# Half of a causal mask moved from VectorE to ScalarE and GpSimd, and a split pair of the last layer put in one buffer

## The chip, the cores and the metric

The kernel runs on one core of one Trainium2 chip. The metric is the device time of one launch in microseconds (us); lower is better. The engines are TensorE (PE, with its weight loads as PEld), VectorE (DVE), ScalarE (ACT), GpSimd (POOL) and SyncE (SP), which issues most DMAs. SBUF is the memory that the engines work in, PSUM the one that TensorE writes.

## The reference, cut to what matters

```python
# 1. linear attention with a decaying state: B, H, S, D = 4, 8, 768, 48
for t in range(S):
    state = alpha[:, :, t, :, None] * state + einsum('bhd,bhe->bhde', k[:, :, t], v[:, :, t])
    y[:, :, t] = einsum('bhd,bhde->bhe', q[:, :, t], state)
# 2. mixture of experts, top 1 of 8: D = 384, F = 1024, N = B*S = 3072 tokens
out[mask] = gate_w[mask, None] * (maximum(x[mask] @ w1[e], 0.0) @ w2[e])
# 3. maxout layer, width 768
return maximum(maximum(x @ w1, x @ w2), x @ w3) @ w_out
```

## The kernel before, in words

Everything runs in one launch, in three stages. In each, the order of the instructions on every engine is the order in which the program text issues them (a manual schedule); what crosses from one engine to another waits on semaphores.

**Attention.** The 3072 tokens are cut into 24 groups `g` of 128 tokens; six groups make one batch, and the state `sbar` is carried from group to group within a batch. The decay is handled by two running products per group, computed on VectorE by scans: `undo` (L290) for the keys and `decay` (L303) for the queries. `decay` then has GpSimd multiply the queries by the product (L305, 112x512, written back to `qt`), and `keys` has VectorE multiply the keys (L316). `spread` (ACT, L311) copies the scaled queries into a block-diagonal tile. `scores(g, hf)` multiplies keys and queries on TensorE for half of the head pairs (`hf` 0 and 1, one PSUM bank `sc` each, 128 keys by 4 heads by 128 queries); `causal(g, hf)` copies this to SBUF as `ss` and sets it to zero where the key comes after the query: one VectorE multiplication by `mask` of 128x512 per half (L345). `sv(g, hf)` multiplies `ss` by the values (L366); `qs(g)` adds what the state gives (L375); `kback` and `update` form the next state, of which VectorE does an addition (L410) and a multiplication (L413), two instructions each. `xev` reads the result (L387 on DVE, L388 and L390 on ACT); `ranges` (ACT, L320) is a check of the products' size.

The loop body of iteration `g` issues, for a later group each: `sv(g, 0)`, `undo(g+3)`, scatters, `sv(g, 1)`, `values(g+2)`, `kback(g+1)`, `spread(g+2)`, `decay(g+3)`, then for both halves `scores(g+1, hf)` and `causal(g+1, hf)`, then `ranges(g+1)`, `keys(g+2)`, `qs(g)`, `xev(g)`, `update(g)`, scatters. So VectorE's order is: scan L290, reciprocal L297, scan L303, both L345, L316, L387, L410, L413. GpSimd's order is: `tokens` (L381, a small copy), a scatter, the query product L305, a scatter. From group 8 on the scatters (L498, indirect DMAs that GpSimd writes) send finished token rows to memory, sorted by expert.

Every second to fourth group a routing chain `route` picks the experts of finished tokens in small VectorE steps spread over an iteration; its one-hot comparison (`oh`, L433) comes right behind `causal`, and TensorE's ranking matmuls (L438) wait for it. In groups 12 to 20 every second iteration also splits expert weights into a rounded part and a rest (`split_w`: ACT L231, L232, POOL L234, DVE L235).

**Experts** (from about 171 us): TensorE multiplies the sorted tokens by each expert's weights, with each operand as a sum of two parts.

**Last layer** (from about 404 us). `x2T` is cut into `BLOCKS` of 256, five times 512, and 256 tokens. `up2(i, f)` computes one of six slices of the hidden layer of block `i`: three groups of nine matmuls (L937 to L939), a copy on ACT (L941), two maxima on DVE (L943), a rounded part `fh` on ACT (L945) and the rest `fl` on GpSimd (L946). `down2(i, q)` multiplies 128 tokens of block `i` by the output weights `wo` (L954 to L956) and scatters the rows (L960). The down part of block `i` runs between the up parts of block `i+1`. The output weights come as 64-bit numbers and are converted by `convert`, a chain of 18 steps (6 weights of 3 steps, L820 to L836 on DVE, ACT and POOL) which are taken two at each `f` of block 0 and three at each `f` of block 1; `down2(0, q)` follows `up2(1, 2)`.

Of the kernel before, what the change touches and what calls it, by code (L numbers as in the profile page):

```python
# [10 lines left out]
F32R = mybir.dt.float32r  # L11
# [4 lines left out]
ALU = mybir.AluOpType  # L16
# [6 lines left out]
C = 128  # L23
# [8 lines left out]
NF2 = F2 // 128  # L32
# [10 lines left out]
TB = 512  # L43
# [16 lines left out]
def fused_kernel(ctx, tc, qT, kT, aT, vn, vf, emb, tau, w1, w2, m1, m2, m3, mo,  # L60
                 gq, gk, ga, gv, out):
    nc = tc.nc
# [75 lines left out]
    for i in range(2):  # L138
        t = wk.tile([HR, WE], F32, tag=f"first{i}", name=f"first{i}", bufs=1)
# [3 lines left out]
    for i in range(3):  # L143
        t = wk.tile([HR, NP, 2, C], F32, tag=f"bdq{i}", name=f"bdq{i}", bufs=1)
# [4 lines left out]
    mask = cst.tile([128, 128], F32, name="mask")  # L149
    nc.gpsimd.memset(mask, 1.0)  # L150
    nc.gpsimd.affine_select(mask, mask, pattern=[[1, 128]], compare_op=ALU.is_ge, fill=0.0,
                            base=0, channel_multiplier=-1)
    sbars = []
    for i in range(2):
        t = wk.tile([HR, H * DE], F32, tag=f"sbar{i}", name=f"sbar{i}", bufs=1)
# [185 lines left out]
    def causal(g, hf):  # L341
        t = cur[g]
        sc = t["sc", hf]
        ss = wk.tile([128, 4, C], F32, tag="ss", name=f"ss_{g}_{hf}", bufs=4)
        nc.vector.tensor_mul(ss, sc.rearrange("p i j t -> p (i j) t"), mask.unsqueeze(1).broadcast_to([128, 4, C]))  # L345
        t["ss", hf] = ss

    def kback(g):
# [145 lines left out]
    def step(it):  # L494
        return next(it, None)
# [131 lines left out]
    with tc.manual_schedule():  # L627
# [18 lines left out]
        embedding_turn(esq)  # L646
        spread(1)
        causal(0, 0)
        causal(0, 1)
        wx = ps_x.tile([128, 512], F32, tag="xp", name="wx")  # L650
        warm(wx, NWARMX)
# [13 lines left out]
        for g in range(NT):  # L665
# [34 lines left out]
            if g + 1 < NT:  # L700
                for hf in range(2):
                    scores(g + 1, hf)
                    causal(g + 1, hf)
                ranges(g + 1)
# [104 lines left out]
    def read_m(src, f):  # L809
        n = f"{src.tensor.name}_{f}"  # L810
        rawm[n] = cvs[-1].tile([128, DM, 2], I32, tag="cr", name=f"cr_{n}", bufs=2)
        nc.sync.dma_start(rawm[n], src[:, f])
# [25 lines left out]
    def convert(ws):  # L838

        for n, w in enumerate(ws):  # L840
            if n + 1 < len(ws):
                read_m(*ws[n + 1][:2])
            for _ in load_m(*w):
                yield
            yield
# [8 lines left out]
    def block(i, pool):  # L854

        w, o = BLOCKS[i], sum(BLOCKS[:i])
        shape = [128, KD, w if i == 0 else TB]
        xh = pool.tile(shape, F32R, tag="bxh", name=f"bxh_{i}")[:, :, 0:w]
        xl = pool.tile(shape, F32R, tag="bxl", name=f"bxl_{i}")[:, :, 0:w]
        for k in range(KD):  # L860
            src = x2T[:, k, o:o + w]
            nc.scalar.copy(xh[:, k], src)
            nc.vector.tensor_sub(xl[:, k], src, xh[:, k].bitcast(F32))
        xsp[i] = (xh, xl)

    with tc.manual_schedule():
        gate_steps = gates()
        conv = convert(todo)
        for s, (u, c) in enumerate(order + [(NU, None)]):
            if s < NA:  # L870
                continue
            e, f = divmod(u, NF1)
# [31 lines left out]
            if e + 1 < E:  # L904
                if u == 1:
                    fetch(1)
                f0 = 5 if e == 0 else 4
# [13 lines left out]
    f2 = fctx.enter_context(tc.tile_pool(name="f2", bufs=2))  # L921
# [7 lines left out]
    def up2(i, f):  # L929
        xh, xl = xsp[i]  # L930
        w = BLOCKS[i]
        t0 = f2.tile([128, TB], F32, tag="t0", name=f"t0_{i}_{f}")[:, 0:w]
        for n in range(3):
            pt = ps_p[n].tile([128, TB], F32, tag="p", name=f"p_{i}_{f}_{n}")[:, 0:w]
            m = mws[n][f]
            for k in range(KD):
                nc.tensor.matmul(pt, m[:, 0, k], xh[:, k], start=(k == 0), stop=False)  # L937
                nc.tensor.matmul(pt, m[:, 1, k], xh[:, k], start=False, stop=False)  # L938
                nc.tensor.matmul(pt, m[:, 0, k], xl[:, k], start=False, stop=(k == KD - 1))  # L939
            if n == 0:  # L940
                nc.scalar.copy(t0, pt)  # L941
            else:
                nc.vector.tensor_tensor(t0, pt, t0, op=ALU.max)  # L943
        hh, hl = (f2.tile([128, TB], F32R, tag=n, name=f"{n}_{i}_{f}", bufs=NF2 + 3)[:, 0:w] for n in ("fh", "fl"))
        nc.scalar.copy(hh, t0)  # L945
        nc.gpsimd.tensor_sub(hl, t0, hh.bitcast(F32))  # L946
        hsp[i, f] = (hh, hl)

    def down2(i, q):
        sl = slice(q * 128, (q + 1) * 128)  # L950
        op = ps_o.tile([128, DM], F32, tag="o", name=f"o_{i}_{q}")
        for f in range(NF2):
            hh, hl = hsp[i, f]
            nc.tensor.matmul(op, hh[:, sl], wo[f][:, 0], start=(f == 0), stop=False)  # L954
            nc.tensor.matmul(op, hh[:, sl], wo[f][:, 1], start=False, stop=False)  # L955
            nc.tensor.matmul(op, hl[:, sl], wo[f][:, 0], start=False, stop=(f == NF2 - 1))  # L956
        t = sum(BLOCKS[:i]) // 128 + q
        ot = f2.tile([128, DM], F32, tag="ot", name=f"ot_{t}", bufs=3)
        nc.scalar.activation(ot, op, AF.Copy, scale=gts[:, t:t + 1])
        nc.gpsimd.indirect_dma_start(out=out, out_offset=bass.IndirectOffsetOnAxis(ap=idx[:, t, 0:1], axis=0),  # L960
                                     in_=ot, in_offset=None, bounds_check=N - 1, oob_is_err=False)

    with tc.manual_schedule():
        nc.sync.dma_start(idx.bitcast(I32), meta[0:N].rearrange("(t p) o -> p t o", p=128))
        nc.vector.memset(gts, 0.0)
        read_m(*todo_o[0][:2])
        block(1, f2)
        conv = convert(todo_o)
        for i in range(NB + 1):
            for f in range(NF2):  # L970
                if i < NB:
                    up2(i, f)
                if i < NB and f < BLOCKS[i] // 128:
                    for t in (sum(BLOCKS[:i]) // 128 + f,):
                        nc.gpsimd.indirect_dma_start(
                            out=gts[:, t:t + 1], out_offset=None, in_=gtok,
                            in_offset=bass.IndirectOffsetOnAxis(ap=idx[:, t, 1:2], axis=0),
                            bounds_check=N - 1, oob_is_err=False)
                for _ in range(2 if i == 0 else 3 if i == 1 else 0):
                    step(conv)  # L980
                if i > 0:
                    f0 = f - 2 if i == 1 else f
                    for q in range(max(0, 2 * f0), min(2 * f0 + 2, BLOCKS[i - 1] // 128)):
                        down2(i - 1, q)
                if f == 3 and 1 < i + 1 < NB:
                    block(i + 1, f2)
        okr = nc.values_load(okv[0:1, 0:1], min_val=0, max_val=128,  # L987
                             skip_runtime_bounds_check_because="a count of 128 flags")
# [159 lines left out]
```

## Time and profile before

| | |
|---|---|
| median of 3 runs (lowest to highest) | 718.27 us (718.24 to 719.01) |
| the profiled execution: its time, its span | 718.81 us, 717.1 us |
| PE, PEld busy | 694.2 us (97%), 634.3 us (88%) |
| DVE, ACT, POOL busy | 433.3 us (60%), 281.8 us (39%), 297.6 us (41%) |

The page cuts the span into 40 slices of 17.9 us; each digit is the busy share in tenths, and PEclk is the granted clock of TensorE in tenths of full speed:

```profile
PE   8999999999999999999999999999999999999994
DVE  8899999897378788888998697211311311303110
ACT  3656566464345444544455323211211212212221
POOL 5312655543124454554555267332333233243331
PEclk9999999899999999999999999999999999999998
```

Slices 0 to 8 are the attention, 9 to 21 the experts, the rest the last layer. A row of a timeline gives start and length in us, engine, line and operation, the tile written and the tiles read, and in brackets how long the engine sat idle before it and what ended that. Consecutive equal instructions are merged (x2), and their lengths overlap a little, since an engine starts the next one before the last has written all. An instruction that is held up after its start shows a greater length, not an idle time.

### The profile page before, as it was taken

The numbers are of one execution on the slowest core, as the hardware profiler recorded it, in microseconds if no ns is written. First come the engines' busy times: TensorE is split into PE (matmuls) and PEld (weight loads), VectorE is DVE, ScalarE is ACT, GpSimd is POOL, SyncE is SP. The second block draws the span as 40 slices with busy tenths as digits, with TensorE's granted clock in tenths as the row PEclk, the third lists the DMA queues.
The fourth block names the chain that finished last, engine by engine and source line by source line (L and its number), as shares of the span: only waits on it lengthen the run. The fifth ranks groups of instructions, "written<-read, shape, count | busy, mean of one in ns | idle before, by whom it ended". The sixth has DMA issues, their size and how long they took to land. (4 is left out here: it accounts for less than half of the span.)

```text
span 717.1 us, 11261 instructions
## 1 busy us (share of the span) xinstructions
PE 694.2 (97%) x4098; PEld 634.3 (88%) x4098; DVE 433.3 (60%) x811; ACT 281.8 (39%) x613; POOL 297.6 (41%) x314
## 2 busy tenths in 40 slices
PE   8999999999999999999999999999999999999994
PEld 4899898899988999999999997888888898898994
DVE  8899999897378788888998697211311311303110
ACT  3656566464345444544455323211211212212221
POOL 5312655543124454554555267332333233243331
PEclk9999999899999999999999999999999999999998
DMA  9999978121355547547454220000000000000000
GB/s 241 287 266 297 321 212 271 53 87 67 108 159 169 146 135 216 173 153 213 148 178 131 46 68 23 23 11 34 1 22 23 1 22 23 1 33 12 12 34 25
DMA packets 32687, 79.69 MB, mean 111 GB/s; under 512 B 8808, under 2 KB 10864, under 8 KB 32624
## 3 DMA queue, kind: packets, MB, share of 16 engines
q1 hardware_dynamic: 28752, 69.40, 33.0%
q0 software_dynamic: 3840, 9.48, 3.5%
q8 instruction: 34, 0.56, 0.3%
q14 instruction: 29, 0.24, 0.1%
q10 hardware_dynamic: 32, 0.01, 0.0%
HBM read 66.97 MB, written 11.90 MB: 110 GB/s over the span
## 5 line engine op out<-in xcount | busy, mean ns | idle before, releaser
L943 DVE TENSOR_TENSOR t<-p,t 128x512 f32<-128x512 f32 (+1 forms) x84 | 51.6, 614 | 198.5 <-PE p L939 195.4
L939 PE MATMUL p<-bxl,m 128*128 128x512 f32 (+1 forms) x378 | 137.0, 362 | 0.0
L937 PE MATMUL p<-bxh,m 128*128 128x512 f32 (+1 forms) x378 | 137.0, 362 | 0.0
L938 PE MATMUL p<-bxh,m 128*128 128x512 f32 (+1 forms) x378 | 137.0, 362 | 0.0
L946 POOL TENSOR_TENSOR fl<-t,fh 128x512 fp32r<-128x512 f32 (+1 forms) x42 | 49.1, 1168 | 153.1 <-ACT fh L945 153.1
L234 POOL TENSOR_TENSOR w<-r,w 128x384 fp32r<-128x384 f32 x64 | 72.3, 1132 | 85.2 <-ACT w L231 85.2
L939 PEld LDWEIGHTS p<-bxl,m 128*128 128x128 f32 x378 | 71.1, 188 | 12.3
L938 PEld LDWEIGHTS p<-bxh,m 128*128 128x128 f32 x378 | 71.1, 188 | 12.0
L937 PEld LDWEIGHTS p<-bxh,m 128*128 128x128 f32 x378 | 71.1, 188 | 11.9
L945 ACT CAST fh<-t 128x512 fp32r<-128x512 f32 (+1 forms) x42 | 23.5, 559 | 146.8 <-DVE t L943 146.8
L590 PE MATMUL h<-xh,w 128*128 128x224 f32 (+8 forms) x207 | 72.1, 348 | 0.0
L591 PE MATMUL h<-xh,w 128*128 128x224 f32 (+8 forms) x207 | 70.4, 340 | 0.3 <-POOL w L234 0.3
L592 PE MATMUL h<-xl,w 128*128 128x224 f32 (+8 forms) x207 | 70.1, 339 | 0.0
L235 DVE TENSOR_TENSOR w<-r,w 128x384 fp32r<-128x384 f32 x64 | 60.3, 942 | 13.4 <-ACT w L232 13.3
L620 PE MATMUL y<-hl,w 128*128 128x464 f32 (+8 forms) x192 | 66.4, 346 | 0.0
L618 PE MATMUL y<-hh,w 128*128 128x464 f32 (+8 forms) x192 | 65.9, 343 | 0.0
L619 PE MATMUL y<-hh,w 128*128 128x464 f32 (+8 forms) x192 | 65.9, 343 | 0.0
L305 POOL TENSOR_TENSOR qt<-qt,PR 112x512 f32<-112x512 f32 x24 | 30.3, 1261 | 67.6 <-DVE PR L303 24.8
L600 ACT ACTIVATE hh<-h 128x464 fp32r<-128x464 f32 (+8 forms) x64 | 32.0, 501 | 61.5 <-PE h L592 61.5
L337 PE MATMUL sc<-bdq,kt 112*128 112x256 f32 x192 | 50.8, 412 | 1.1 <-POOL hm L184 1.1
L366 PE MATMUL xp<-vt,ss 128*128 128x56 f32 x384 | 47.1, 276 | 3.8 <-ACT jk L320 2.4
L955 PE MATMUL o<-wo,fh 128*128 128x384 f32 x144 | 48.5, 337 | 1.5 <-POOL wo L836 1.5
(205 smaller groups left out, 1445.9 us busy)
## 6 DMA issues: line engine op xcount, KB each, us to landing
r<-in_w SPq DMA_DIRECT2D x64, 384.0 KB, 3.7
cr_in_m<-in_m SPq DMA_DIRECT2D x18, 384.0 KB, 4.8
at<-in_aT SPq DMA_DIRECT2D x11, 451.9 KB, 10.7
kt<-in_kT SPq DMA_DIRECT2D x11, 448.0 KB, 10.6
qt<-in_qT SPq DMA_DIRECT2D x11, 448.0 KB, 9.1
vt<-in_vn SPq DMA_DIRECT2D x11, 448.0 KB, 7.9
ft<-in_vf SPq DMA_DIRECT2D x11, 384.0 KB, 6.9
exr<-xs_scratch SPq DMA_DIRECT2D x5, 675.5 KB, 7.8
```

The lines of the kernel that those rows point to most:

```text
L234: nc.gpsimd.tensor_sub(a[:, 1], r1[:, k], a[:, 0].bitcast(F32))
L235: nc.vector.tensor_sub(b[:, 1], r2[:, k], b[:, 0].bitcast(F32))
L590: nc.tensor.matmul(hp, a[:, 0, k], t["xh"][:, k, c], start=(k == 0), stop=False)
L591: nc.tensor.matmul(hp, a[:, 1, k], t["xh"][:, k, c], start=False, stop=False)
L592: nc.tensor.matmul(hp, a[:, 0, k], t["xl"][:, k, c], start=False, stop=(k == KD - 1))
L618: nc.tensor.matmul(y, w[:, 0, sl], hh, start=(f == 0 and c.start == 0), stop=False, skip_group_check=True)
L619: nc.tensor.matmul(y, w[:, 1, sl], hh, start=False, stop=False, skip_group_check=True)
L620: nc.tensor.matmul(y, w[:, 0, sl], hl, start=False, stop=(f == NF1 - 1), skip_group_check=True)
L937: nc.tensor.matmul(pt, m[:, 0, k], xh[:, k], start=(k == 0), stop=False)
L938: nc.tensor.matmul(pt, m[:, 1, k], xh[:, k], start=False, stop=False)
L939: nc.tensor.matmul(pt, m[:, 0, k], xl[:, k], start=False, stop=(k == KD - 1))
L943: nc.vector.tensor_tensor(t0, pt, t0, op=ALU.max)
```

## The change: what it does

Two things are changed. First, from group 1 on, the second half of a group's scores (`hf` 1) is no longer multiplied by the mask on VectorE: ScalarE copies the PSUM bank to `ss`, and GpSimd then sets the upper triangle to zero in place by `affine_select`, an operation that keeps an element where an expression of partition and position is not negative. The first half, and both halves of group 0, stay on VectorE. In program order the copy stands on ScalarE between `spread(g+2)` and `ranges(g+1)`, and the selection on GpSimd between the query product of `decay(g+3)` and the next scatter.

Second, in the last layer both parts of the hidden tiles of block 0 (256 columns each) lie in one `fh` tile of 512 columns. `fh` gets 10 buffers where it had 9, `fl` 7 where it had 9. The conversion of the output weights takes two steps at each `f` of block 1 where it took three, and `down2(0, q)` comes behind `up2(1, 3)` where it came behind `up2(1, 2)`.

```diff
--- before.py
+++ after.py
@@ -342,7 +342,13 @@
         t = cur[g]
         sc = t["sc", hf]
         ss = wk.tile([128, 4, C], F32, tag="ss", name=f"ss_{g}_{hf}", bufs=4)
-        nc.vector.tensor_mul(ss, sc.rearrange("p i j t -> p (i j) t"), mask.unsqueeze(1).broadcast_to([128, 4, C]))
+        sc = sc.rearrange("p i j t -> p (i j) t")
+        if hf == 0 or g == 0:
+            nc.vector.tensor_mul(ss, sc, mask.unsqueeze(1).broadcast_to([128, 4, C]))
+        else:
+            nc.scalar.copy(ss, sc)
+            nc.gpsimd.affine_select(ss, ss, pattern=[[0, 4], [1, C]], compare_op=ALU.is_ge, fill=0.0, base=0,
+                                    channel_multiplier=-1)
         t["ss", hf] = ss
 
     def kback(g):
@@ -941,7 +947,11 @@
                 nc.scalar.copy(t0, pt)
             else:
                 nc.vector.tensor_tensor(t0, pt, t0, op=ALU.max)
-        hh, hl = (f2.tile([128, TB], F32R, tag=n, name=f"{n}_{i}_{f}", bufs=NF2 + 3)[:, 0:w] for n in ("fh", "fl"))
+        fh = f2.tile([128, TB], F32R, tag="fh", name=f"fh_{i}_{f}", bufs=NF2 + 4)
+        if 2 * w <= TB and i == 0:
+            hh, hl = fh[:, 0:w], fh[:, w:2 * w]
+        else:
+            hh, hl = fh[:, 0:w], f2.tile([128, TB], F32R, tag="fl", name=f"fl_{i}_{f}", bufs=NF2 + 1)[:, 0:w]
         nc.scalar.copy(hh, t0)
         nc.gpsimd.tensor_sub(hl, t0, hh.bitcast(F32))
         hsp[i, f] = (hh, hl)
@@ -976,10 +986,10 @@
                             out=gts[:, t:t + 1], out_offset=None, in_=gtok,
                             in_offset=bass.IndirectOffsetOnAxis(ap=idx[:, t, 1:2], axis=0),
                             bounds_check=N - 1, oob_is_err=False)
-                for _ in range(2 if i == 0 else 3 if i == 1 else 0):
+                for _ in range(2 if i < 2 else 0):
                     step(conv)
                 if i > 0:
-                    f0 = f - 2 if i == 1 else f
+                    f0 = f - 3 if i == 1 else f
                     for q in range(max(0, 2 * f0), min(2 * f0 + 2, BLOCKS[i - 1] // 128)):
                         down2(i - 1, q)
                 if f == 3 and 1 < i + 1 < NB:
```

## Rows read from the trace of the kernel before

**Rows 1.** Busy us by window: PE, PEld, DVE, ACT, POOL; PEclk, DMA, GB/s
```profile
24.00:160.00 136.00, 129.50 (x1001) 123.20 (x1001) 128.13 (x265) 83.51 (x192) 59.17 (x63) 0.96 0.75 224
122.00:126.00 4.00, 4.00 (x16) 3.41 (x15) 3.84 (x10) 2.58 (x6) 0.25 (x1) 0.57 0.96 357
135.00:143.00 8.00, 8.00 (x38) 7.25 (x38) 5.03 (x13) 3.99 (x9) 6.28 (x7) 0.57 0.28 101
600.00:660.00 60.00, 60.00 (x277) 50.72 (x276) 13.55 (x19) 13.82 (x26) 19.39 (x17) 1.00 0.04 14
```

**Rows 2.** Timeline of VectorE through one group without routing
```profile
34.85 1.29 DVE L345 TENSOR_TENSOR ss<-sc,mask 128x512 f32<-128x512 f32 x2
36.05 0.70 DVE L316 TENSOR_TENSOR kt<-kt,PR 112x512 f32<-112x512 f32 x1
...
38.65 1.23 DVE L290 TENSOR_TENSOR_SCAN PR<-at,last 112x516 f32<-112x516 f32 x1 [0.20 <-DVE sbar L413]
...
40.13 1.23 DVE L303 TENSOR_TENSOR_SCAN PR<-at,first 112x516 f32<-112x516 f32 x1
41.39 1.29 DVE L345 TENSOR_TENSOR ss<-sc,mask 128x512 f32<-128x512 f32 x2
```

**Rows 3.** Timeline of TensorE, the two value products of the same stretch
```profile
36.34 1.90 PE L366 MATMUL xp<-vt,ss 128*128 128x56 f32 x16
...
42.55 1.90 PE L366 MATMUL xp<-vt,ss 128*128 128x56 f32 x16
```

**Rows 4.** Timeline of GpSimd, the query product of the same stretch
```profile
41.44 1.19 POOL L305 TENSOR_TENSOR qt<-qt,PR 112x512 f32<-112x512 f32 x1 [5.23 <-DVE PR L303]
```

**Rows 5.** Timelines of VectorE and GpSimd where a query product came late
```profile
73.67 0.95 DVE L433 TENSOR_TENSOR oh<-fi,sm 128x32 bf16<-128x32 f32 x1
...
80.43 1.18 POOL L305 TENSOR_TENSOR qt<-qt,PR 112x512 f32<-112x512 f32 x1 [2.64 <-PE xp L375]
...
81.33 0.82 DVE L316 TENSOR_TENSOR kt<-kt,PR 112x512 f32<-112x512 f32 x1
```

**Rows 6.** Instructions of line 345: shortest, median, longest ns, first and last start
```profile
L345 DVE TENSOR_TENSOR ss<-sc,mask x48: 675/684/693, 13.4 to 166.7; 128x512 f32<-128x512 f32 x48
```

**Rows 7.** Timelines of GpSimd and VectorE, two GpSimd instructions in a row (experts)
```profile
307.44 1.01 POOL L836 TENSOR_TENSOR m<-v_in_m,v_in_m 128x384 fp32r<-128x384 f32 x1
...
307.56 1.31 DVE L235 TENSOR_TENSOR w<-r,w 128x384 fp32r<-128x384 f32 x1 [0.23 <-ACT w L232]
...
308.41 1.33 POOL L234 TENSOR_TENSOR w<-r,w 128x384 fp32r<-128x384 f32 x1
```

**Rows 8.** Timelines of VectorE and GpSimd, the second of two selections (start)
```profile
3.79 1.71 DVE L290 TENSOR_TENSOR_SCAN PR<-at,last 112x516 f32<-112x516 f32 x1 [0.88 <-DMA at<-in_aT]
...
4.13 0.28 POOL L151 TENSOR_SCALAR_AFFINE_SELECT mask<-mask 128x128 f32<-128x128 f32 x1
```

**Rows 9.** GpSimd by line and form: busy us, mean ns, idle before
```profile
L305 POOL TENSOR_TENSOR qt<-qt,PR 112x512 f32<-112x512 f32 x24 | 30.3, 1261 | 67.6 <-DVE PR L303 24.8 <-DVE sm L431 13.6 <-PE sc L337 8.7
...
L151 POOL TENSOR_SCALAR_AFFINE_SELECT mask<-mask 128x128 f32<-128x128 f32 x1 | 0.3, 283 | 0.0
...
L186 POOL TENSOR_SCALAR_AFFINE_SELECT hm<-hm 128x24 f32<-128x24 f32 x1 | 0.2, 213 | 0.1
```

**Rows 10.** ScalarE by line and form, from 410 to 700 us
```profile
L941 ACT COPY t<-p 128x512 f32<-128x512 f32 x30 | 17.5, 585 | 24.4 <-PE p L939 24.4
```

**Rows 11.** Timeline of TensorE, three of its gaps in the attention
```profile
74.67 0.22 PE L438 MATMUL rk<-oh,ones_b 128*128 128x24 bf16 x3 [0.86 <-DVE oh L433]
...
119.86 1.96 PE L366 MATMUL xp<-vt,ss 128*128 128x56 f32 x16 [0.94 <-issue]
...
134.36 2.39 PE L366 MATMUL xp<-vt,ss 128*128 128x56 f32 x16 [1.09 <-ACT jk L320]
```

**Rows 12.** Timelines of VectorE and TensorE, the last conversion and the first down2
```profile
441.19 1.53 DVE L825 SCALAR_TENSOR_TENSOR ex_in_mo<-ex_in_mo,sg_in_mo 128x384 int32<-128x384 int32 x1
...
446.54 0.44 PE L955 MATMUL o<-wo,fh 128*128 128x384 f32 x1 [1.45 <-POOL wo L836]
```

## The prediction

> **What bounds the kernel now.** I read the slices of the page first: TensorE is busy in nine tenths or more of nearly every slice, VectorE only in the first nine. Then busy time by window, for the attention alone: in 136 us TensorE sits idle for 6.5 (129.50 busy) and VectorE for 7.9 (128.13 busy) [rows 1]. Both are nearly full, so I laid their timelines side by side. With all inputs there, TensorE needs 42.55 - 36.34 = 6.21 us for a group [rows 3], VectorE 41.39 - 34.85 = 6.54 us [rows 2]. VectorE is the slower by 0.33 us, but it starts ahead and skips the state work at the end of each batch; so TensorE runs without a gap for some groups, then meets a VectorE that is late, and waits: 0.86, 0.94 and 1.09 us are three of these waits [rows 11]. After two of them TensorE's granted clock was 0.57 on average, over 4 and over 8 us [rows 1], a mix of 2.4 GHz and a stretch at 1.2; that cost 4 x 0.43 + 8 x 0.43 = 5.1 us of TensorE's work. Behind the attention TensorE sets the time, with one hole in the last layer of 1.45 us, where the first down2 waits for the last converted weights [rows 12].
>
> **The change, VectorE's side.** Call T the end of the L303 scan (41.36) [rows 2]. Before, the two masks run from T+0.03, 0.645 us each (half of 1.29), the keys L316 from T+1.23 to T+1.93 (34.82 to 36.05 and 36.75) [rows 2]. 23 masks of 0.645 us leave VectorE, 14.8 us in all. If that came free, VectorE's group would take 5.9 us and TensorE's 6.21 would rule.
>
> It does not come free. GpSimd's query product starts at T+0.08 and lasts 1.19 [rows 4]: it lies exactly beside the two masks. The masks never felt it, 675 to 693 ns in all 48 [rows 6]; their scores come from PSUM. The keys, whose operands are both in SBUF, do feel it: where the product came late (80.43 to 81.61), they took 0.82 us instead of 0.70 and ended 0.54 us after the product's end; the one-hot comparison, also with two SBUF operands, once took 0.95 [rows 5]. So with one mask gone the keys are issued at T+0.65, stand until the product (T+0.08 to T+1.27) is nearly through and end at 1.27 + 0.54 = T+1.81. VectorE wins 0.12 us a group, not 0.645. 21 of the 23 selections have a query product ahead of them; of these one iteration waits for TensorE anyway and in two the product came late; 18 x 0.12 = 2.2 us.
>
> The Trainium skill, page "SBUF — State Buffer", section "Who interferes with whom", has this as a rule against the change: a VectorE instruction with two SBUF inputs and a GpSimd instruction that reads SBUF share one read interface, and whichever comes second waits for the whole of the first. The trace agrees, by the 0.82 us above. By the rule the gain is the 2.2 us; without it TensorE's limit would rule and the 6.5 us of idle time could go.
>
> **The other engines.** ScalarE gets 23 copies of 128x512 from PSUM; the same form costs 0.585 us [rows 10], 13.5 us in all. The scores' second half is complete before T in a group that VectorE limits, so the copy is done before GpSimd has finished the query product. Behind it on ScalarE wait L320, which nobody on the path needs, and L388, which waits for VectorE anyway; ScalarE is busy 83.5 of 136 us [rows 1]. I cost it at nothing; if L388 came late, the 0.6 us would go to a scatter.
>
> GpSimd gets 23 selections of 128x512. The trace has none of that size: 0.213 us for 24 columns and 0.283 for 128 [rows 9], 0.67 ns a column, so 0.283 + 384 x 0.67 ns = 0.54; four times the 128 columns gives 1.13, the two-operand product of nearly this size 1.19 [rows 4]. I take 0.6, nearest to the same operation's own slope, and keep 0.54 to 1.19. The selection reads SBUF too. In the one clean case of VectorE waiting while GpSimd had a second instruction right behind the first, VectorE went between: L235 waited for L836 and ended at 308.87, and L234, issued at 308.41, took 1.33 instead of about 1.0 [rows 7]. So the selection comes after the keys' reads, from T+1.67 to T+2.27, beside L387 and L410, which read PSUM. GpSimd's queue behind it (scatter, `tokens`, the weight rest of split groups, scatter) moves back 1.0 us at most; it is busy 59 of 136 us [rows 1], and 14 us more leave it room before the next query product.
>
> **TensorE's side.** In a group that VectorE limits, the first half of `sv` starts at about T+0.85 and the second at T+1.8; now the second waits for the selection, T+2.3. So such a gap moves by VectorE's accumulated gain less 0.5 us. Group by group: the gap before group 6 gives +0.1 (VectorE ahead by 0.4 to 0.5 after routing in group 4). In group 8, where a late product held the one-hot comparison (the 0.95 us of rows 5), that hold goes and I put VectorE 1.1 us earlier; the gap before group 11 then gives -0.6, before 16 -0.9, before 18 -1.1, the last one-hot wait -0.4 more. Sum: about -1.5 us of the 2.2. The clock's two low stretches I leave as they are.
>
> **Last layer.** Six conversion steps now spread over three `f` of block 1 instead of two, and their user comes one up2 later. The last two steps took 441.19 to 446.54, 5.35 us [rows 12]; the last pair now starts when `up2(1, 2)` is through, and TensorE has `up2(1, 3)` (27 matmuls) and 15 of down2 to do first, 42 x 60/277 = 9.1 us [rows 1]. The 1.45 us go, and nothing on TensorE's path behind gives them back: -1.45. The bounds are 0 (another wait takes its place) and -1.45. The new buffers: `fh` holds six of block 0 and four of block 1, so `up2(1, 4)` finds one free as down2 of block 0 is done by then. With 7 `fl` GpSimd has to wait at `up2(i, 1)` until `down2(i-1, 3)` has begun; behind it are gathers and scatters with a whole block to spare. Nothing.
>
> **Sum.** On the profiled execution: 718.81 (span 717.1 and 1.7 around it) - 1.5 - 1.45 = 715.9. The median shown is 0.54 lower: 715.3 us. Its own range is 713.5 to 717.2: attention -0.3 to -3.3.
>
> **Rivals.**
> *GpSimd keeps the read port (slower).* If the selection follows the product at once, the keys stand until T+1.27+0.54+0.6 = T+2.35, 0.42 later than before; 18 groups give +7.6, with -1.45 that is 724.4 us. For it: the first scan of the kernel took 1.71 us instead of 1.23, ending at 5.50, so it started 0.14 before the end of the second of two selections in a row [rows 8]; it had let both pass. Against it: rows 7, and that this scan's start may not be the time at which it asked. Each group that goes this way costs 0.54 against the forecast; from the sixth of 18 the kernel is no faster than before.
>
> *TensorE runs through (faster).* If shorter waits keep the clock up, the 5.1 us come back: 710.2. For it: the low stretches follow the longest waits of all, and the one of 0.86 was followed by none (slice 4 of the page). Against: the waits only shrink by half a microsecond or move between the two halves of `sv`. If VectorE also got its 0.645 us, the 6.5 us of idle time would go and 705 is the floor.
>
> *The selection is long (no change).* With 1.19 us it ends at T+2.86. From a group's first `sv` to the second half two groups on, TensorE needs 6.21 + 0.87 = 7.1 us; VectorE takes 41.36 - 36.75 = 4.6 us from its keys to T [rows 2], so the selection would end 4.6 + 2.9 = 7.5 us after the state product: some 0.4 us per two groups in the stretches without gaps, some 2 us, and 0.6 at each gap. Attention +1.5, in all 718.3 us.
>
> **Chances.** Forecast 0.46, GpSimd keeps the port 0.22, TensorE runs through 0.19, long selection 0.13. About 0.2% (1.44 us) is what a measurement can tell from no change, so "faster" is below 716.83: nearly all of the forecast (0.41), the fast rival (0.19) and 0.02 of the long selection, 0.62; within 0.2% the rest of the forecast and most of the long selection, 0.15; slower 0.23. The range 709 to 722 takes in the fast rival's 710.2 and two thirds of the way to the slow one's 724.4.
>
> **What would show it.** L316 longer than 0.9 us from its issue, ending 0.5 us after L305: the port. L345 at 25 instead of 48, 0.68 each. The selection starting as L316 ends: right; L316 ending 0.5 us after the selection: the slow rival. Idle time of TensorE inside `sv`, ahead of its second eight matmuls. Windows from 120 to 143 us at clock 1.0: the fast rival. No wait for L836 at the first down2. The prediction is wrong if the keys take 0.7 us beside the product, or if GpSimd's scatters push the query product past T.

## The result and the profile after

The changed kernel takes 724.34 us (median of 16 runs, 719.70 to 728.74), the kernel before in the same runs 718.30 (715.27 to 723.43): a ratio of 1.0075 [1.0048, 1.0103]. By that ratio it is slower by 5.4 us, where 715.3 was forecast and 722 was the upper end of the range. The profiled execution took 725.98 us with a span of 724.3.

First the busy time by window (PE, PEld, DVE, ACT, POOL; then TensorE's granted clock, DMA share, GB/s). The first window is the attention, the last holds the end of the weight conversion in the last layer. Kernel after:

```profile
24.00:160.00 136.00, 129.26 (x937) 121.51 (x936) 118.49 (x224) 90.20 (x200) 72.56 (x79) 0.92 0.71 213
60.00:68.00 8.00, 7.96 (x36) 7.29 (x37) 3.90 (x6) 3.19 (x9) 2.23 (x3) 0.57 0.86 271
128.00:136.00 8.00, 8.00 (x37) 7.28 (x37) 5.55 (x13) 3.62 (x9) 1.95 (x3) 0.57 0.58 212
144.00:153.00 9.00, 8.52 (x44) 7.78 (x44) 5.83 (x14) 4.65 (x11) 7.17 (x8) 0.62 0.19 68
440.00:500.00 60.00, 60.00 (x285) 51.64 (x284) 23.65 (x35) 15.17 (x27) 26.28 (x23) 1.00 0.06 21
```

One more window, ahead of most of these, after and before:

```profile
16.00:26.00 10.00, 8.51 (x42) 7.66 (x41) 6.14 (x11) 3.98 (x9) 4.76 (x7) 0.66 1.03 286
16.00:26.00 10.00, 8.86 (x60) 8.03 (x58) 7.96 (x15) 4.63 (x12) 4.37 (x6) 0.83 1.03 282
```

TensorE is as busy as before, 129.26 us of 136 against 129.50 [rows 1], yet finishes less: 937 matmuls are recorded against 1001. The column that differs is the clock, 0.92 against 0.96. Three stretches of 8 to 9 us lie near 0.6, a mix of 2.4 and 1.2 GHz, where before there were two, of 4 and 8 us [rows 1]. Summed over windows of 2 us from 0 to 170, (1 - clock) times their length is 13.7 us, against 6.8 before: 6.9 us of TensorE's work lost on top. The low stretches hold 5.1 of it (8 x 0.43 + 8 x 0.43 + 9 x 0.38 = 10.3 us against 4 x 0.43 + 8 x 0.43 = 5.2 before), and 16 to 26 us holds 1.7 (10 x 0.34 against 10 x 0.17). This last part can't be put down to the change: the clock had fallen by 20 us, the first selection starts at 25.28, and no value product had waited for one. In the slices of the page the same shows as four 8s in PEclk over the first ten slices, where before there was one, while PE stays near 9:

```profile
PE   8999999899999999999999999999999999999994
PEclk9898999889999999999999999999999999999998
```

The first matmul of the experts started at 180.4 us instead of 171.5: 8.9 us later. From there to the first matmul of the last layer nothing is lost or won (403.8 became 412.7), and the last layer gives 1.7 back. So the whole loss lies in the attention. Of the 8.9 us, 1.7 are the clock of the first 26 us and 5.1 the clock of the low stretches behind. TensorE's idle time up to the experts is only 0.9 us longer (11.2 against 10.3, and 0.35 of it in one wait for a DMA, 1.49 us instead of 1.14, at 18.98). The 1.2 us left are busy time. A block of `sv` that is cut in two takes 1.07 + 1.10 us by its rows below, the sixteen in one 1.90 [rows 3], and nine blocks are cut: by this estimate enough for the rest, but not tried by itself.

Now VectorE and GpSimd in that stretch, from their timelines in the kernel after. VectorE, an early group (37.44), an ordinary one (42.58 to 44.45), and two in a row (92.69 to 99.11):

```profile
37.44 1.77 DVE L316 TENSOR_TENSOR kt<-kt,PR 112x512 f32<-112x512 f32 x1
...
42.58 1.23 DVE L303 TENSOR_TENSOR_SCAN PR<-at,first 112x516 f32<-112x516 f32 x1
43.84 0.69 DVE L347 TENSOR_TENSOR ss<-sc,mask 128x512 f32<-128x512 f32 x1
44.45 1.18 DVE L316 TENSOR_TENSOR kt<-kt,PR 112x512 f32<-112x512 f32 x1
...
92.69 0.69 DVE L347 TENSOR_TENSOR ss<-sc,mask 128x512 f32<-128x512 f32 x1
...
99.11 0.69 DVE L347 TENSOR_TENSOR ss<-sc,mask 128x512 f32<-128x512 f32 x1
```

GpSimd, the early and the ordinary group:

```profile
36.89 1.19 POOL L305 TENSOR_TENSOR qt<-qt,PR 112x512 f32<-112x512 f32 x1 [4.75 <-DVE PR L303]
38.02 0.64 POOL L350 TENSOR_SCALAR_AFFINE_SELECT ss<-ss 128x512 f32<-128x512 f32 x1
...
43.90 1.18 POOL L305 TENSOR_TENSOR qt<-qt,PR 112x512 f32<-112x512 f32 x1 [4.65 <-DVE PR L303]
45.03 1.10 POOL L350 TENSOR_SCALAR_AFFINE_SELECT ss<-ss 128x512 f32<-128x512 f32 x1
```

The ordinary group is the forecast's. The scan L303 ends at T = 43.81. The keys L316 start at 44.45, stand beside the query product L305 (it ends at 45.08) and are through at 45.63, T + 1.82. The selection L350 is issued at 45.03 and shows 1.10 us instead of 0.64, because it lets the keys pass. At 37.44 it went the other way: the keys took 1.77 us and waited for the selection too.

TensorE, the value products of that ordinary group (44.64) and of two others, in brackets its idle time ahead and what ended that:

```profile
44.64 1.07 PE L372 MATMUL xp<-vt,ss 128*128 128x56 f32 x8
46.18 1.10 PE L372 MATMUL xp<-vt,ss 128*128 128x56 f32 x8 [0.47 <-POOL ss L350]
...
58.43 1.07 PE L372 MATMUL xp<-vt,ss 128*128 128x56 f32 x8 [0.95 <-ACT jk L320]
60.04 1.96 PE L372 MATMUL xp<-vt,ss 128*128 128x56 f32 x8 [0.54 <-POOL ss L350]
...
142.88 1.07 PE L372 MATMUL xp<-vt,ss 128*128 128x56 f32 x8 [1.05 <-ACT jk L320]
144.48 1.17 PE L372 MATMUL xp<-vt,ss 128*128 128x56 f32 x8 [0.53 <-POOL ss L350]
```

Before, these sixteen matmuls ran as one block [rows 3]. Now the second eight wait for the selection, and in some groups the first eight have waited just before. The row names ScalarE's L320, whose result `sv` does not read; what it does read, VectorE's mask, began at 57.64 in the group of 58.43 and ended at 58.32, just before L320 did. In this execution two of the three low stretches follow such a pair: 0.95 + 0.54 us ahead of the one at 60, 1.05 + 0.53 ahead of the one at 144. The eight matmuls at 60.04 take 1.96 us instead of 1.07. The third, at 128, follows a pair of 0.42 + 0.47.

Four lines of the kernel after, by their source (shortest, median and longest ns, first and last start), answer to [rows 6, 10]:

```profile
L316 DVE TENSOR_TENSOR kt<-kt,PR x24: 660/1166/1768, 7.0 to 170.2; 112x512 f32<-112x512 f32 x24
L350 POOL TENSOR_SCALAR_AFFINE_SELECT ss<-ss x23: 626/812/1173, 25.3 to 176.4; 128x512 f32<-128x512 f32 x23
L349 ACT COPY ss<-sc x23: 586/586/587, 24.6 to 175.7; 128x512 f32<-128x512 f32 x23
L347 DVE TENSOR_TENSOR ss<-sc,mask x25: 673/690/692, 13.4 to 174.8; 128x512 f32<-128x512 f32 x25
```

In the kernel before, the keys' line was:

```profile
L316 DVE TENSOR_TENSOR kt<-kt,PR x24: 660/684/819, 7.0 to 162.1; 112x512 f32<-112x512 f32 x24
```

### The profile page after: what moved, and what is told of

It reads as the page before. It is cut to its first block, busy times and chain, and to the rows that moved or that the text cites. A ratio compares the mean times of both kernels' runs of the same rounds, so it can differ in the third digit from the quotient of the medians.

```text
span 724.3 us, 11278 instructions
## 1 busy us (share of the span) xinstructions
PE 701.9 (97%) x4098; PEld 641.0 (88%) x4098; DVE 432.0 (60%) x788; ACT 294.7 (41%) x636; POOL 319.2 (44%) x337
## 5 line engine op out<-in xcount | busy, mean ns | idle before, releaser
L956 POOL TENSOR_TENSOR fl<-t,fh 128x512 fp32r<-128x512 f32 (+1 forms) x36 | 43.5, 1209 | 138.8 <-ACT fh L955 103.5
L372 PE MATMUL xp<-vt,ss 128*128 128x56 f32 x384 | 50.1, 280 | 6.5 <-POOL ss L350 3.8
L372 PEld LDWEIGHTS xp<-vt,ss 128*128 128x128 f32 x384 | 46.8, 195 | 8.9 <-POOL ss L350 5.0
L305 POOL TENSOR_TENSOR qt<-qt,PR 112x512 f32<-112x512 f32 x24 | 30.1, 1255 | 55.1 <-DVE PR L303 22.1
L337 PE MATMUL sc<-bdq,kt 112*128 112x256 f32 x192 | 52.7, 424 | 1.4 <-POOL hm L184 1.4
```

Source lines behind the costliest of these rows:

```text
L372: nc.tensor.matmul(t["xp"][:, h * DE:(h + 1) * DE], t["ss", hf][:, 2 * (p % 2) + j], t["v"][:, h * DE:(h + 1) * DE], start=(h == 0), stop= ...
```

## The experiments

Theory: the second half of `sv` now waits for the selection; behind such waits, above all where one for VectorE in the same group precedes it, TensorE's clock falls to 1.2 GHz for some microseconds, and most of the loss is this clock. Rivals: GpSimd keeps the read port, so that the keys and VectorE are late (the prediction's slow rival, whose 724.4 us is nearly what was measured); the last layer's part costs something; or the selection's wait alone is the loss, with no clock in it. All times are medians of 11 or 12 runs (e8: 6), and each ratio is to the kernel before run on the same chip.

**The last layer's part alone (e1).** The mask's lines go back, the rest stays:

```
+        nc.vector.tensor_mul(ss, sc.rearrange("p i j t -> p (i j) t"), mask...)   # both halves
-        if hf == 0 or g == 0: ... else: copy, affine_select
```

> The last layer's part alone, with both masks on VectorE as before. Both theories: the 1.45 us hole at the first down2 is gone and nothing replaces it, so -1.3 to -1.7 us against the kernel before, and an attention stage like before's (first expert matmul at about 171.5 us, granted clock as before's).

**The mask's part alone (e2).** The lines of the last layer go back.

> The masks' part alone. Both theories: +7 to +9 us against the kernel before, all of it ahead of the first expert matmul, and the 1.45 us hole still there. Clock theory (the new wait inside the value product lets TensorE's clock fall more often): mean granted clock about 0.978 against before's 0.985. Port theory (VectorE, held at L316, sets a longer group): a group takes over 6.5 us of VectorE where its clock is full.

e1 took 715.67 us, ratio 0.9968 [0.9938, 0.9998]; e2 724.31, ratio 1.0066 [1.0038, 1.0094]. The two parts have opposite signs, and the loss is the mask's. Its 4.7 us (2.7 to 6.8) are fewer than the 7 to 9 expected; the mean clock was 0.982, against 0.987 before. Window 440 to 500 tells of the wait at the first down2, e1 first, then e2:

```profile
440.00:500.00 60.00, 60.00 (x287) 51.92 (x286) 14.64 (x22) 13.92 (x24) 23.83 (x22) 1.00 0.05 20
```

```profile
440.00:500.00 60.00, 58.29 (x273) 49.67 (x273) 22.13 (x35) 14.70 (x26) 26.80 (x24) 1.00 0.06 21
```

With the last layer's part TensorE does not stop in these 60 us; without it 1.71 us are idle, and they are the wait of [rows 12].

**The mask's part without the selection (e3).** The last layer is that of before. The upper triangle of the second half's scores is not zeroed, so this kernel leaves out a step of the computation:

```
             nc.scalar.copy(ss, sc)
-            nc.gpsimd.affine_select(ss, ss, ...)
```

> The masks' part alone, with GpSimd's selection left out (the second half keeps its upper triangle; scores above the diagonal are not set to zero). The keys still stand behind the query product. Clock theory: the wait ahead of the second half of the value product is gone, the clock stays up as before or better, and the time falls to 712 to 718 us. Port theory: L316 still ends 0.5 us after L305, and the time stays within 2 us of the masks' part alone.

It took 716.86 us, ratio 0.9969 [0.9945, 0.9994]. The selections, as they lie in e2, cost 724.31 - 716.86 = 7.5 us. Its keys' line:

```profile
L316 DVE TENSOR_TENSOR kt<-kt,PR x24: 661/1175/1427, 6.4 to 158.9; 112x512 f32<-112x512 f32 x24
```

The keys are held as long as in the kernel after (median 1175 ns, 1166 there) and the kernel is still a little faster than before. So the hold of the keys by the query product is not the loss. The 7.5 us are 0.33 us for each of the 23 selections, which any of the theories could claim; the next runs part them.

**The keys ahead of the mask (e4).** The changed kernel, with one block moved:

```
+            if g < NT - 2:
+                keys(g + 2)
             if g + 1 < NT:
                 for hf in range(2): scores(g + 1, hf); causal(g + 1, hf)
```

> The changed kernel with the keys' product L316 issued ahead of the first mask, so that the query product, which comes a moment later, waits 0.6 us for it instead of holding it up. Port theory: VectorE wins 0.5 us a group, TensorE's 6.21 us rule, 709 to 714 us. Clock theory: the first half of the value product starts 0.6 us later after the scan and the second right behind it, so one wait instead of two; if VectorE is early enough for both, about 712 us with a clock above 0.985, if not, as the changed kernel (722 to 725).

**The selection ahead of the query product (e5).** The changed kernel, with GpSimd's product taken out of `decay` into `queries(g)`, and issued behind the group's selection:

```
                 ranges(g + 1)
+            if g + 3 < NT:
+                queries(g + 3)
```

> The changed kernel with GpSimd's selection issued ahead of the query product instead of behind it. The second half of the value product then finds its scores ready at about T+1 instead of T+2.3. Clock theory (what costs is TensorE's wait for the selection inside the value product, and the low clock behind such waits): these waits go, mean clock back at 0.986 or more, 715 to 719 us. Port theory (VectorE, held at L316, sets the time): L316 waits for the product all the same, and now for the selection too in some groups; no gain, 722 to 727 us.

e4 took 716.24 us, ratio 0.9966 [0.9941, 0.9991]; e5 717.24, ratio 0.9987 [0.9962, 1.0012]. Either order takes back 7 to 8 us of the change's 724.3 with the same instructions. In e4 neither expectation was met in size: 716.24 lies between the two, at a clock of 0.988. What they share is when the second half is ready. In e4 (timelines of VectorE, GpSimd and TensorE):

```profile
102.35 1.23 DVE L303 TENSOR_TENSOR_SCAN PR<-at,first 112x516 f32<-112x516 f32 x1
103.55 0.68 DVE L316 TENSOR_TENSOR kt<-kt,PR 112x512 f32<-112x512 f32 x1
...
103.66 1.62 POOL L305 TENSOR_TENSOR qt<-qt,PR 112x512 f32<-112x512 f32 x1 [1.94 <-DVE pos L455]
105.24 0.63 POOL L350 TENSOR_SCALAR_AFFINE_SELECT ss<-ss 128x512 f32<-128x512 f32 x1
...
104.94 2.08 PE L372 MATMUL xp<-vt,ss 128*128 128x56 f32 x16
```

Now the keys have the port first and the query product stands (1.62 us instead of 1.19). The selection ends at 105.87, and TensorE, which started the first eight at 104.94, runs all sixteen without a stop. In e5 the selection (L354 there) is ahead of the product (L309), and an ordinary group looks like this:

```profile
97.78 0.68 DVE L351 TENSOR_TENSOR ss<-sc,mask 128x512 f32<-128x512 f32 x1
98.47 0.68 DVE L320 TENSOR_TENSOR kt<-kt,PR 112x512 f32<-112x512 f32 x1
...
98.64 1.01 POOL L354 TENSOR_SCALAR_AFFINE_SELECT ss<-ss 128x512 f32<-128x512 f32 x1 [0.88 <-ACT ss L353]
99.63 1.18 POOL L309 TENSOR_TENSOR qt<-qt,PR 112x512 f32<-112x512 f32 x1
...
98.71 2.10 PE L376 MATMUL xp<-vt,ss 128*128 128x56 f32 x16
```

Again the second half is there when TensorE comes to it. With the product behind the selection the keys mostly ran free as well: over 0.9 us in 5 of 24 groups, against 15 in the kernel after. So these two runs alone don't part the keys' hold from the wait in `sv`; e3 does, whose keys were held in 15 of 24 groups without the loss. What is left is the wait inside `sv`. Its line from 24 to 165 us (busy, mean ns, idle time and what ended it) in the kernel after and in e4:

```profile
L372 PE MATMUL xp<-vt,ss 128*128 128x56 f32 x320 | 42.0, 281 | 6.5 <-POOL ss L350 3.8 <-ACT jk L320 2.4
```

```profile
L372 PE MATMUL xp<-vt,ss 128*128 128x56 f32 x342 | 42.2, 275 | 4.1 <-ACT jk L320 2.4 <-POOL ss L350 0.8 <-issue 0.7
```

In e5 the idle time of its line (L376) is 3.9 us. So it shrinks by some 2.5 us in both, less than half of the 7 to 8 us of time. The rest would be the clock: 0.97 in both from 24 to 160 us, 0.92 in the kernel after.

**The waits stay, and TensorE works in them (e6).** The changed kernel with idle matmuls of zeros, 128x512 bf16, ahead of those `sv` blocks that wait. They give nothing to the result and make nothing ready earlier:

```
+FILL = ({6: 4, 12: 2, 16: 2, 18: 4}, {g: 2 for g in (4, 6, 10, 11, 12, 14, 16, 18, 20)})
+        for _ in range(FILL[hf].get(g, 0)):
+            nc.tensor.matmul(t["xp"], wsrc[:, 0:128], wsrc, start=(hf == 0), stop=True, ...)
```

> The changed kernel with 2 to 4 idle matmuls (zeros, 128x512 bf16, about 0.21 us each) in TensorE's queue ahead of the first half of the value product of groups 6, 12, 16, 18 and 2 ahead of the second half of groups 4, 6, 10, 11, 12, 14, 16, 18, 20, where the trace shows it waiting. They fill waits and shorten none. Clock theory: the clock no longer falls behind these groups, 0.987 or more against 0.980, and 4 to 6 us come back: 718 to 720 us. If the low clock only goes along with the slowdown: clock and time as the changed kernel, 723 to 726 us.

It took 719.05 us, ratio 1.0005 [0.9978, 1.0033], against 1.0075 [1.0048, 1.0103] without them; the mean falls from 724.12 to 719.35, by 4.8 us, and the mean clock over the runs rises from 0.980 to 0.990. The window of the attention:

```profile
24.00:160.00 136.00, 130.92 (x987) 120.38 (x995) 124.93 (x233) 92.51 (x206) 77.49 (x83) 0.97 0.75 218
```

From 24 us on, the clock fell once in this execution, right behind its longest wait, one that had no idle matmuls (2.39 us for the selection, ahead of the second half at 144.78).

Added work on the engine that sets the time made the kernel faster. That separates the clock from the wait. Not all of the 4.8 us need be the mask's, since waits ahead of a first half, which e6 fills too, stood in the kernel before as well; what filling them is worth there, the next run tells.

**The same in the kernel before (e7).** There the long waits stand ahead of the first half:

```
+FILL = ({6: 2, 11: 2, 12: 3, 16: 4, 18: 4}, {})
```

> The kernel before with 2 to 4 such idle matmuls ahead of the value products of groups 6, 11, 12, 16 and 18, the longest waits there that are not for the one-hot comparison. Clock theory: the two low stretches behind groups 16 and 18 go in most executions, mean clock from 0.987 to 0.991, -2 to -4 us. Otherwise: no change, or +1 us where the matmuls last longer than the wait.

717.45 us, ratio 0.9978 [0.9954, 1.0002]: at best a small gain, less than the 2 to 4 us expected, and its interval takes in 1. By the means it is 1.5 us (718.93 to 717.40), so some 3.3 to 4.8 us of the mask's loss are the clock (an estimate; the intervals are about 2 us to either side). The clock over the runs rose from 0.9875 to 0.9907; the low stretches that are left follow TensorE's waits for the one-hot comparisons of routing (1.25, 1.25 and 0.82 us), which this run did not fill.

**The selection twice (e8).** The changed kernel with each selection issued a second time:

```
+            for _ in range(2):
                 nc.gpsimd.affine_select(ss, ss, ...)
```

> The changed kernel with each selection done twice in a row (the second changes nothing), which delays the second half of the value product by another 0.64 us. Clock theory: waits inside the value product of about 1.1 us instead of 0.5, more low stretches, clock below 0.975, 729 to 735 us. If the selection mattered only through the port: L316 held in the same way (it goes between two selections), 724 to 727 us.

734.24 us, ratio 1.0219 [1.0175, 1.0263]. The clock went lower than in the kernel after by little, 0.977 against 0.980 over the runs. The idle time of `sv` took most of it:

```profile
L373 PE MATMUL xp<-vt,ss 128*128 128x56 f32 x296 | 41.2, 286 | 15.3 <-POOL ss L351 12.9 <-ACT jk L320 1.8 <-issue 0.3
```

15.3 us instead of 6.5: 8.8 of the 9.9 us between the medians of the two kernels. The expectation that the clock would carry the next step failed. Each 0.63 us of a longer selection comes out as 9.9/23 = 0.43 us, nearly all as plain waiting. So the first step, from no wait to a short one, cost mostly clock, the second hardly any.

**The best of both (e9, e10).** e9 is e1 with e7's idle matmuls, and more of them ahead of the ranking matmuls of five routing chains; e10 is e4 with a few of each kind:

```
+FILLR = {0: 4, 1: 3, 3: 4, 4: 2, 5: 3}     # e9, beside e7's FILL
+        for _ in range(FILLR.get(i, 0)):
+            nc.tensor.matmul(rk, wsrc[:, 0:128], wsrc, start=True, stop=True, ...)
```

> The last layer's part alone, with idle matmuls ahead of the value products of groups 6, 11, 12, 16, 18 and ahead of the ranking matmuls of five routing chains, so that TensorE's longest waits of the attention are filled. Clock theory: mean clock 0.991 or more against 0.987, 712.5 to 715 us, below the last layer's part alone (715.7). Otherwise: 715 to 717.

> The changed kernel with L316 ahead of the first mask, and idle matmuls where that kernel's trace shows TensorE waiting (value products of groups 1, 6, 16, 18, two routing chains). Clock theory: clock 0.991 or more against 0.9875, 713 to 715 us against 716.2. Otherwise: 716 to 717.5.

e9 took 713.97 us, ratio 0.9928 [0.9900, 0.9956]; e10 714.43, ratio 0.9929 [0.9904, 0.9954]. Both beat the kernel before by 5 us and the changed one by 10, and can't be told apart. The attention in e9:

```profile
24.00:160.00 136.00, 132.24 (x1029) 122.91 (x1037) 130.68 (x266) 85.41 (x196) 61.38 (x65) 1.00 0.82 225
```

The clock is 1.00 through the whole stretch. e9's busy time holds the idle matmuls, so its 132.24 is not all work.

## Why the prediction was wrong, step by step

**The read port: right.** T + 1.81 was forecast for the end of the held keys, T + 1.82 was measured. The Trainium skill's rule of the page "SBUF — State Buffer", section "Who interferes with whom", holds in this trace from both sides: the keys stand for the product in the kernel after (1.18 us instead of 0.68), the product for the keys in e4 (1.62 instead of 1.19). VectorE's group came to 99.11 - 92.69 = 6.42 us, as 6.54 - 0.12 had said. At 6.42 VectorE is still the slower of the two, as TensorE needs 6.21.

**The prices: right.** Copy 0.586 us (forecast 0.585), selection 0.63 to 0.64 us where nothing holds it (0.6), mask 0.69. The second half of `sv` started at 46.18, T + 2.37 (T + 2.3).

**The last layer: right.** No wait at the first down2, and e1's ratio of 0.9968 is 2.3 us with an interval from 0.1 to 4.5, which holds the 1.45.

**"The clock's two low stretches I leave as they are": this step failed.** They became three: 5.1 us more in the profiled execution, 3.3 to 4.8 us by e6 and e7. The prediction had the new wait of half a microsecond inside `sv`, had its sign and place, and added it up as time alone. It argued that "the waits only shrink by half a microsecond or move between the two halves of `sv`", and read that as a reason why the clock would not get better; that a wait split in two could make it worse was in none of the cases. In the profiled execution groups 10, 11 and 12, with waits of 0.54, 0.29 and 0.48 us ahead of the second half only, were followed by no low stretch; groups 6, 16 and 18, with a wait ahead of each half, were. Other executions don't keep to this, as the end of this section tells.

**The attention's sum of "about -1.5 us": it did not come either.** It was a sum of waits, and TensorE's idle time up to the experts grew by 0.9 us instead. `sv` waits 6.5 us from 24 to 165, against 3.8 before (here its line in the kernel before):

```profile
L366 PE MATMUL xp<-vt,ss 128*128 128x56 f32 x352 | 43.1, 276 | 3.8 <-ACT jk L320 2.4 <-issue 0.9 <-DVE ss L345 0.5
```

Of that, 3.8 us are waits for the selection, and those for VectorE (2.4) did not shrink in return. The gain of VectorE that I had carried from group to group arrived at the ranking matmuls, which wait for the one-hot comparison, and not in `sv`. From 24 to 165 us they wait 0.3 us for it (L444), where before it was 2.6:

```profile
L438 PE MATMUL rk<-oh,ones_b 128*128 128x16 bf16 (+3 forms) x20 | 1.9, 170 | 2.7 <-DVE oh L433 2.6
```

In `sv` the gap at group 6, forecast 0.1 longer, went from 0.46 us to 0.95 + 0.54, and that at group 18 from 1.09 to 1.05 + 0.53. In the routing groups the selection also goes between the one-hot comparison and the keys, as here on VectorE and GpSimd of the kernel after:

```profile
51.07 0.60 DVE L439 TENSOR_TENSOR oh<-fi,sm 128x32 bf16<-128x32 f32 x1
51.59 1.16 DVE L316 TENSOR_TENSOR kt<-kt,PR 112x512 f32<-112x512 f32 x1
...
50.44 1.19 POOL L305 TENSOR_TENSOR qt<-qt,PR 112x512 f32<-112x512 f32 x1 [4.18 <-DVE sm L437]
51.57 0.64 POOL L350 TENSOR_SCALAR_AFFINE_SELECT ss<-ss 128x512 f32<-128x512 f32 x1
```

The comparison waited out the product, and the selection was next in turn before the keys asked. What each of these waits is worth was not tried by itself.

**The slow rival had the number and not the cause.** "GpSimd keeps the read port" gave 724.4 us from 18 groups in which the keys wait for the selection. One ordinary group did so (37.44, 1.77 us), and two routing groups (51.59 and 80.21, 1.16 us each). Its terms were also added up wrongly: T+1.27+0.54+0.6 is T+2.41 and not T+2.35, which over 18 groups gives 725.5 us. e3 leaves the keys behind the product, without the loss. **The fast rival was the right question with the wrong sign:** that the clock hangs on TensorE's waits is what e6 and e9 show. e9 is nearest to what it described, the clock at 1.00 through the attention, reached by filling the waits and without the mask's change. One more sum of the prediction is off: with -0.3 for the attention the upper end of its own range is 716.5, not 717.2.

What stays open: which wait the clock falls behind. In the profiled execution of e2, with the same mask code, a low stretch came behind one wait alone (0.53 us; the clock was 0.57 from 100 to 102 and 0.58 from 102 to 104):

```profile
99.06 1.10 PE L372 MATMUL xp<-vt,ss 128*128 128x56 f32 x8 [0.53 <-POOL ss L350]
```

In e8 a pair of 0.51 + 1.17 us (at 133.50 and 135.73) was followed by none, and in e1 neither was a wait of 1.39 us (at 133.72). So a pair of waits is not the condition, and no run varied one wait by itself.

## What to carry to other kernels

Where one engine is nearly full, a short new wait of that engine can cost more than its length if its clock falls behind it; so read the granted clock of every stretch that follows a wait, and count every new wait as a risk to the clock, not only as its own length. When an operation goes to a second engine, its place in that engine's queue counts more than the time it frees: the same instructions in another order (e4, e5) gave back the whole loss. Where a wait can't be moved, idle matmuls in it are a cheap trial that also tells clock from wait.

## What the runs showed of the hardware

- TensorE's clock fell to 1.2 GHz behind waits of less than 1.1 us each, and stayed there for some 3.4 to 6.9 us of nearly full work (4 and 8 us at a mean of 0.57): at 60 us behind 0.95 + 0.54, while 7.96 of the next 8 us were busy. Not every such wait was followed by it. The Trainium skill, page "TensorE: Matmul & The Clock Gate", section "A second HAM failure mode: psum-queue depth-cycling", tells of a kernel in which short idle times between groups of matmuls, coming often enough, make the clock swing between its levels; this trace agrees, with three such swings behind the waits of `sv`.
- Matmuls of zeros hold the clock: 0.980 became 0.990 over the runs in e6, and 0.987 became 0.995 from e1 to e9.
- Executions of one kernel differ by several us (715 to 724 for the kernel before), and the clock goes with it: over 35 executions of the kernel before it lay between 0.978 and 0.992, and 0.001 of it went with 0.5 us. A difference of 2 us between two kernels needs many runs here, and one profiled execution does not stand for a kernel's clock: that of e3 was at 0.981, with four low stretches in the attention, where e3's mean is 0.989.
- Of two engines that want the read port, the one that waits mostly goes between two instructions of the other (the selection of 1.10 us at 45.03), but not always (37.44), and not when it comes after the other's second one (51.59).
